# Phases rounded in PSUM, operands and background loads moved earlier, convolution strips in thirds

## The chip, the cores and the metric

One core of a Trainium2 chip (trn2) runs the kernel. The metric is the device time of one execution in microseconds (us). Line numbers in the profiles (L159) are those of the kernel profiled; the changed kernel has other numbers than the kernel before.

TensorE multiplies a stationary operand, loaded as weights, with a moving operand and writes to PSUM. ScalarE (ACT in the profile) does activations, VectorE (DVE) element-wise work, GpSimd (POOL) some element-wise work and, like SyncE (SP), issues DMA. An engine executes and issues in the order of its program: the timeline under e4 shows a store that is ready and leaves 4.8 us later, behind loads that wait. That order was set by a scheduler when the kernel was built, from the program order and the dependences.

## The reference, cut to what matters

Eight batches, a sequence of S = 5696, 128 channels:

```python
y = irfft(rfft(x, n=2*S) * rfft(h, n=2*S))[:, :S, :]     # a causal convolution per channel
theta = y @ w_theta
zr, zi = y * cos(theta), y * sin(theta)
u = y + einsum('ts,bsd->btd', w_tok_r, zr) + einsum('ts,bsd->btd', w_tok_i, zi)
out = u + relu(u @ w_ch)
```

The kernel computes the convolution as matmuls with Toeplitz strips of h. Then the *phases*: theta, its sine and cosine, zr and zi, for 45 tiles of 128 rows, of which 22 come first and 23 run in the background of the next stage. Then come the two 5696 x 5696 products, in a scheme with seven products in place of eight, in two passes over the sequence. Each pass works on *pairs* of output row tiles and keeps eleven *right operands* (zr and zi with five VectorE sums each) in SBUF. A pair is 154 matmuls of width 512 in four *stretches*; one piece of background work fits into each stretch.

## The kernel before: the parts that matter

The convolution: two strips per channel, four buffers.

```python
for k0, k1 in ((0, KS), (KS, NT)):                       # KS = 23, NT = 45
    strip = csb.tile([P, KS * P + 64], BF16, tag="strip")  # pool of 4
    nc.sync.dma_start(strip[:64, :w + 64], ...)            # 64 shifted rows of h_pad
    nc.vector.tensor_copy(strip[64:, :w], strip[:64, 64:w + 64])
    for k in range(k0, k1):
        nc.tensor.matmul(psum[...], strip[:, c:c + P], x_sb2[:, d, :B * ntj], ...)
```

The phases. `w_theta` is divided by 2 pi beforehand, so theta counts turns. Adding and taking away MAGIC = 1.5 * 2^23 rounds to whole turns and brings the argument of the sine into one turn:

```python
nc.tensor.matmul(theta_ps[...], yT[:, b, :], w_theta_sb, start=True, stop=True)   # per batch b
nc.scalar.activation(red, theta_ps, AF.Identity, bias=magic)                # theta + MAGIC
nc.vector.scalar_tensor_tensor(red, red, MAGIC, theta_ps, subtract, subtract)
nc.scalar.activation(mag, red, AF.Abs)
nc.scalar.activation(red, red, AF.Sin, ..., scale=-TWO_PI)                  # sine
nc.scalar.activation(mag, mag, AF.Sin, bias=half_pi, scale=-TWO_PI)         # cosine
zi_eng.tensor_mul(zi, red, yflat); nc.vector.tensor_mul(zr, mag, yflat)     # zi lies in red, zr in mag
for z, dst in ((zr, zr_hbm), (zi, zi_hbm)):
    nc.sync.dma_start(dst[ti]..., z)
```

All eleven right operands are loaded after the 22 tiles, 88 loads on SyncE. A background phase loads its `yb` in the slot that uses it, into one buffer, and TensorE transposes it at once. In pass two the four addends of a pair use four fixed buffers, from which the output is also stored:

```python
def first():                                   # background, third group of a stretch
    yb = cp.tile([P, 4, D], BF16, tag="yb")    # one buffer
    nc.sync.dma_start(yb..., half(y2_hbm, t, h))
    phases_a(yb, 0, yT, mps, 1)                # four transposes
...
c = cp.tile([P, 512], F32, tag=f"c{k}")        # addend and result, k = 0..3
```

## Time and profile before

| | before |
|---|---|
| median of 2 runs | 2746.23 us (2744.26 to 2748.20) |
| span of the profiled run | 2729.5 us |
| TensorE busy, granted clock | 83% of the span, 0.930 |
| VectorE, GpSimd, ScalarE busy | 61%, 31%, 23% |

This is the view of stretches for the kernel before. A line covers one stretch of time (from:to, its length), then for TensorE matmuls, weight loads, VectorE, ScalarE and GpSimd the busy us and the number of instructions, then the granted clock of TensorE, the busy share of the DMA engines and GB/s.

```profile
core 0: us, PE busy (x) PEld busy (x) DVE busy (x) ACT busy (x) POOL busy (x), PEclk, DMA share, GB/s
105.00:663.00 558.00, 484.56 (x5755) 410.61 (x5756) 230.67 (x256) 227.35 (x129) 0.00 (x0) 0.99 0.73 173
663.00:793.00 130.00, 40.99 (x365) 32.60 (x363) 89.56 (x98) 104.16 (x112) 17.34 (x32) 0.54 0.69 215
793.00:863.00 70.00, 46.70 (x162) 15.16 (x161) 51.93 (x94) 3.25 (x5) 14.27 (x25) 0.91 0.87 186
863.00:1811.00 948.00, 807.47 (x3727) 363.29 (x3726) 596.63 (x1121) 153.06 (x237) 442.23 (x757) 0.93 0.72 125
1811.00:1884.00 73.00, 47.86 (x159) 15.69 (x159) 52.15 (x98) 0.00 (x0) 17.19 (x32) 0.86 0.93 201
1884.00:2730.00 846.00, 792.02 (x4128) 373.22 (x4127) 578.10 (x1115) 102.66 (x180) 356.71 (x664) 0.99 0.74 126
```

The stretches are: the convolution; from its end to the first matmul of the first pair; the first pair; the rest of pass one; the first pair of pass two; the rest. (The load of x fills the first 105 us and is not touched by the change.) TensorE is meant to be the limit, but the second line has it busy for 41 of 130 us at clock 0.54, and the fourth for 807 of 948.

In the fourth, the loss lies where the background phases run (863 to 1440 us, eleven pairs). First the list of waits of TensorE there (who waited for whom; us in total, times, longest), then that stretch alone:

```profile
PE tpz L172 <- DMA yb<-y_hbm: 126.5, 42, 4.7
```

```profile
863.00:1440.00 577.00, 448.14 (x2056) 201.30 (x2056) 345.04 (x619) 146.26 (x225) 239.82 (x390) 0.89 0.63 116
```

The transposes wait 126.5 us for yb, and the clock is down to 0.89. The convolution's groups of instructions (count after the x, busy us, mean ns, then the idle time before them and who ended it) show TensorE waiting for the strips:

```profile
L159 PE MATMUL psum<-x_sb,strip 128*128 128x360 bf16 x5753 | 483.7, 244 | 73.4 <-DVE strip L148 37.4 <-DVE strip L154 34.7 <-ACT x_sb L119 1.1
```

The phases are carried by ScalarE. It is busy 104 of the 130 us, in 22 tiles with four ops of about 1.1 us each:

```profile
L191 ACT ACTIVATE red<-red,zero_b 128x1024 f32<-128x1024 f32 x22 | 25.0, 1138 | 0.1
L192 ACT ACTIVATE mag<-mag,half_pi 128x1024 f32<-128x1024 f32 x22 | 25.0, 1135 | 0.0
L186 ACT ACTIVATE red<-theta_ps,magic 128x1024 f32<-128x1024 f32 x22 | 24.0, 1108 | 12.6 <-DMA zi_hbm<-red 10.1 <-PE theta_ps L183 2.6
L190 ACT ACTIVATE mag<-red 128x1024 f32<-128x1024 f32 x22 | 22.5, 1047 | 1.3 <-DVE red L187 1.3
```

And in pass two, the chain of work that ended last (start, duration, what) goes in most pairs through an output store, the load of the next addend into the same buffer, and VectorE. One pair end as an example, then TensorE's busy time over 400 us of that pass:

```profile
by line: DMA out_dram<-c_19077 29.1%; DMA c_19442<-cp_hbm 17.1%; issue 6.6%; PE m_19803 L492 5.4%; DVE c_19077 L359 4.6%; DVE c_19446 L509 4.5%; PE m_19439 L492 4.4%; DVE c_19444 L511 4.1%; DVE c_19083 L359 4.0%; DVE c_19442 L510 4.0%; DVE 
...
2178.89 0.70 DVE c_19077 L359
...
2179.61 4.37 DMA out_dram<-c_19077
...
2183.99 2.57 DMA c_19442<-cp_hbm
...
2191.47 0.61 DVE c_19444 L511
...
2192.12 0.81 PE m_19803 L492 x3
```

```profile
2000.00:2400.00 400.00, 381.30 (x1985) 178.61 (x1985) 283.37 (x548) 48.61 (x85) 181.85 (x339) 1.00 0.79 133
```

### The profile page before, as it was taken

How to read it: one execution, taken by the hardware profiler on the slowest of the kernel's cores; microseconds unless marked ns; L12 is line 12 of the kernel's file. 1: busy time of each engine (PE TensorE's matmuls, PEld its weight loads, DVE VectorE, ACT ScalarE, POOL GpSimd, SP SyncE). 2: the span in 40 equal slices, each digit the busy share in tenths (PEclk: the TensorE clock that was granted, in tenths of full speed). 3: DMA queues.
4: the chain of work that ended last, by engine and by line, in shares of the span. 5: the costliest groups of instructions: out<-in, count | busy, mean ns of one | idle time of the engine just before them, and what ended most of it. 6: DMA issues, size and time to landing. Idle time of an engine off the chain costs nothing.

```text
span 2729.5 us, 38700 instructions
## 1 busy us (share of the span) xinstructions
PE 2269.4 (83%) x14422; PEld 1220.2 (45%) x14422; DVE 1663.5 (61%) x2842; ACT 636.6 (23%) x708; POOL 851.6 (31%) x1520
## 2 busy tenths in 40 slices
PE   4688888887347887777779999987999999999997
PEld 1377777776212333333334444433444444444443
DVE  5544434434767665565556677767776777667774
ACT  3444344435841222222220000000111111111111
POOL 0000000001002444344335655533444544444440
PEclk7699999999569998888889999999999999999998
DMA  9977777767858666566658978888777877787772
GB/s 249 225 179 176 171 178 175 177 169 181 263 158 165 116 133 118 105 114 120 107 105 138 154 129 133 134 167 172 132 130 135 140 126 133 129 138 134 129 131 61
DMA packets 431004, 404.64 MB, mean 148 GB/s; under 512 B 64480, under 2 KB 368864, under 8 KB 430688
## 3 DMA queue, kind: packets, MB, share of 16 engines
q0 software_dynamic: 222816, 131.33, 38.1%
q1 hardware_dynamic: 207568, 269.20, 36.4%
q8 instruction: 114, 1.87, 0.3%
q10 hardware_dynamic: 432, 1.64, 0.2%
q14 instruction: 74, 0.61, 0.1%
HBM read 448.22 MB, written 85.02 MB: 195 GB/s over the span
## 4 chain that ended last, share of the span: by engine, by line
PE 47%; DMA 28%; DVE 12%; ACT 4%; issue 4%; SPq 3%; POOL 1%; DVEq 0%; ACTq 0%; POOLq 0%
PE psum L159 10%; DMA strip<-h_pad 8%; DMA yb<-y_hbm 8%; DMA tmp<-in_x_dram 3%; SPq L258 2%; DVE mag L197 1%; DVE wt L284 1%; ACT red L191 1%; ACT mag L192 1%; DVE strip L148 1%; ACT mag L190 1%; ACT red L186 1%; PE tpz L172 1%; DVE strip L154 1%; PE utp L350 1%
## 5 line engine op out<-in xcount | busy, mean ns | idle before, releaser
L275 POOL DMA_DIRECT2D wb<-in_moe_w_tok_r_dram x720 | 388.5, 547 | 874.3 <-PE psum L159 659.5
L275 POOL DMA_DIRECT2D wb<-in_moe_w_tok_i_dram x720 | 388.9, 547 | 625.5 <-DVE wt L284 586.4
L159 PE MATMUL psum<-x_sb,strip 128*128 128x360 bf16 (+44 forms) x5760 | 483.9, 244 | 73.4 <-DVE strip L148 37.4
L159 PEld LDWEIGHTS <-strip 128*128 128x128 bf16 x5760 | 410.7, 98 | 147.3 <-DVE strip L148 43.8
L284 DVE STREAM_TRANSPOSE wt<-wb 128x384 f32<-128x384 f32 (+1 forms) x720 | 365.7, 527 | 162.9 <-DMA wb<-in_moe_w_tok_i_dram 25.7
L492 PEld LDWEIGHTS <-wt 128*128 128x128 bf16 x1936 | 191.9, 100 | 256.0 <-issue 40.9
L163 ACT ACTIVATE y_sb<-psum 128x360 bf16<-128x360 f32 x128 | 227.5, 1778 | 330.4 <-PE psum L159 330.4
L148 DVE COPY strip<-strip 64x2944 bf16<-64x2944 bf16 (+1 forms) x128 | 115.3, 904 | 164.4 <-DMA strip<-h_pad 148.9
L154 DVE COPY strip<-strip 64x2944 bf16<-64x2944 bf16 (+1 forms) x128 | 115.4, 906 | 160.5 <-DMA strip<-h_pad 141.3
L352 ACT ACTIVATE uts<-utp 128x512 bf16<-128x512 bf16 (+1 forms) x90 | 53.3, 592 | 571.1 <-PE utp L350 571.1
L196 POOL TENSOR_TENSOR red<-red,yb 128x512 bf16<-128x512 f32 x46 | 56.5, 1229 | 283.7 <-ACT red L191 274.6
L176 ACT ACTIVATE yT<-tpz 128x512 bf16<-128x512 bf16 x68 | 39.7, 594 | 420.3 <-PE tpz L172 420.3
L172 PE MATMUL tpz<-ident_bf,yb 128*128 128x128 bf16 x184 | 22.9, 263 | 126.7 <-DMA yb<-y_hbm 126.5
L187 DVE SCALAR_TENSOR_TENSOR red<-red,theta_ps 128x512 f32<-128x512 f32 (+1 forms) x68 | 58.0, 857 | 63.2 <-ACT red L186 62.8
L117 PE MATMUL rps<-tmpbf,R_bf 128*128 128x512 bf16 x90 | 46.5, 620 | 53.8 <-DVE tmpbf L114 53.5
L183 PE MATMUL theta_ps<-w_theta_sb,yT 128*128 128x128 bf16 x360 | 49.3, 284 | 50.1 <-ACT yT L176 47.2
L172 PEld LDWEIGHTS <-yb 128*128 128x128 bf16 x184 | 13.1, 113 | 149.5 <-DMA yb<-y_hbm 149.0
L114 DVE CAST tmpbf<-tmp 128x1024 bf16<-128x1024 f32 x45 | 56.5, 1261 | 34.5 <-DMA tmp<-in_x_dram 32.8
L347 ACT ACTIVATE ub<-c_16588 128x512 bf16<-128x512 f32 x1 | 0.6, 630 | 325.7 <-DVE c_16588 L511 325.7
L186 ACT ACTIVATE red<-theta_ps,magic 128x512 f32<-128x512 f32 (+1 forms) x68 | 55.6, 824 | 62.5 <-PE theta_ps L183 52.5
L183 PEld LDWEIGHTS <-yT 128*128 128x128 bf16 x360 | 33.7, 129 | 77.3 <-ACT yT L176 58.6
L190 ACT ACTIVATE mag<-red 128x512 f32<-128x512 f32 (+1 forms) x68 | 51.6, 766 | 37.7 <-DVE red L187 37.7
(6264 smaller groups left out, 4212.4 us busy)
## 6 DMA issues: line engine op xcount, KB each, us to landing
strip<-h_pad SPq DMA_DIRECT2D x128, 376.0 KB, 4.2
strip<-h_pad SPq DMA_DIRECT2D x128, 360.0 KB, 5.0
wb<-in_moe_w_tok_r_dram POOLq DMA_DIRECT2D x352, 96.0 KB, 4.4
wb<-in_moe_w_tok_i_dram POOLq DMA_DIRECT2D x352, 96.0 KB, 4.6
wb<-in_moe_w_tok_r_dram POOLq DMA_DIRECT2D x352, 80.0 KB, 4.1
wb<-in_moe_w_tok_i_dram POOLq DMA_DIRECT2D x352, 80.0 KB, 3.6
tmp<-in_x_dram SPq DMA_DIRECT2D x44, 512.0 KB, 5.8
y_hbm<-y_sb SPq DMA_DIRECT2D x45, 256.0 KB, 5.2
```

The costliest lines, as they stand in the source:

```text
L148: nc.vector.tensor_copy(strip[64:, :w], strip[:64, 64:w + 64])
L154: nc.vector.tensor_copy(strip[:64, 64:w + 64], strip[64:, :w])
L159: nc.tensor.matmul(psum[:, B * k: B * k + B * ntj], strip[:, c:c + P], x_sb2[:, d, :B * ntj], start=(k == 0), stop=(k == NT - 1))
L163: nc.scalar.activation(y_sb[:, :, :, d].rearrange("q t b -> q (t b)"), psum, AF.Copy)
L172: nc.tensor.transpose(tpz[:, b, :], y_ap[:, q + b, :], ident_bf)
L183: nc.tensor.matmul(theta_ps[:, b * D:(b + 1) * D], yT[:, b, :], w_theta_sb, start=True, stop=True)
L186: nc.scalar.activation(red, theta_ps, AF.Identity, bias=magic)
L187: nc.vector.scalar_tensor_tensor(red, red, MAGIC, theta_ps, op0=ALU.subtract, op1=ALU.subtract)
L190: nc.scalar.activation(mag, red, AF.Abs)
L275: nc.gpsimd.dma_start(wb[32 * i:32 * i + 32, :ng, :nj * 64], bass.AP(tensor=a.tensor, offset=a.offset + row0 * S + p * H + i * QR + j0 * 6 ...
L284: nc.vector.transpose(wt.rearrange("p j t r -> p (j t r)").bitcast(F32).rearrange("p (j g t) -> p g j t", j=TJ, g=4)[:, :ng, :nj], wb[:, : ...
L492: nc.tensor.matmul(ms[q], a[q][:, j, :, r], bts[jj][:, r, q, :], start=(jj == 0 and r == 0), stop=(jj == NJ - 1 and r == 1 and q not in left))
```

## The change

The change wants to take five kinds of waiting from TensorE at once. The convolution uses thirds of a strip and six buffers. For the first 22 tiles TensorE adds MAGIC, adds theta, takes MAGIC away and takes theta away again, all accumulated in PSUM, which removes one ScalarE op and one VectorE op per tile. The first four right operands get SBUF of their own and are loaded during the phases; of the other seven, ScalarE's queue issues half the loads. yb is loaded one slot ahead into two buffers. In pass two the addends rotate through six buffers. Two more moves go with it: the stores of y2 are issued by GpSimd, and the short pair of pass one moves from its end to its middle.

```diff
-    KS = 23
+    KS = 15
-    with tc.tile_pool(name="conv_sbuf", bufs=4) as csb, \
+    with tc.tile_pool(name="conv_sbuf", bufs=6) as csb, \
-            for k0, k1 in ((0, KS), (KS, NT)):
+            for k0 in range(0, NT, KS):
 ...
+            ones, plus, minus, w_neg = turns          # ones [1,128]; plus, minus [1,512] = +-MAGIC
+            for q in range(0, nb, 4):
+                bank = theta_ps[:, q * D:(q + 4) * D]
+                nc.tensor.matmul(bank, ones, plus, start=True, stop=False)
+                for b in range(q, q + 4):
+                    nc.tensor.matmul(theta_ps[:, b * D:(b + 1) * D], yT[:, b, :], w_theta_sb, start=False, stop=False)
+                nc.tensor.matmul(bank, ones, minus, start=False, stop=False)
+                for b in range(q, q + 4):
+                    nc.tensor.matmul(theta_ps[:, b * D:(b + 1) * D], yT[:, b, :], w_neg, start=False, stop=(b == q + 3))
+            r = theta_ps
+        nc.scalar.activation(mag, r, AF.Abs)
+        nc.scalar.activation(red, r, AF.Sin, bias=zero_b, scale=-TWO_PI)
 ...
+    def load_b(p, j, pool):
+            for z, s0, eng in ((zr_hbm, M2, nc.sync), (zi_hbm, M7, nc.sync if j < NE else nc.scalar)):   # NE = 4
 ...
-            nc.sync.dma_start(y2_hbm[ti], y_ap)
+                nc.gpsimd.dma_start(y2_hbm[ti], y_ap)
+            for j in range(max(0, 2 * a - 3), min(NE, 2 * a - 1)):      # after each round of tiles
+                load_b(0, j, bpe)
 ...
+            def load():
+                st["yb"] = yb = ybp.tile([P, 4, D], BF16, tag="yb", name="yb")   # pool of 2
+                nc.sync.dma_start(yb.rearrange("p b d -> p (b d)"), half(y2_hbm, t, h))
 ...
+            if p == 1:
+                tag = ("c0", "c1", "c2", "c3", "red", "mag")[tags["n"] % 6]
 ...
+        pairs = (list(range(11)) + [None] + list(range(11, 22)), list(range(22)) + [None])
 ...
-                    first, second = spread.pop(0)
+                    _, first, second = spread.pop(0)
                     first()
+                    if spread:
+                        spread[0][0]()                 # the load of the next slot
```

More of the change, by code (lines that the diff above doesn't have):

```diff
@@ L40 @@
     HW = Sp + P
-    KS = 23
+    KS = 15
+    assert NT % KS == 0
     BD = B * D
@@ L138 @@
             psum = cps.tile([P, NT * B], F32, tag="convps")
-            for k0, k1 in ((0, KS), (KS, NT)):
-                w = (k1 - k0) * P
+            for k0 in range(0, NT, KS):
+                k1 = k0 + KS
+                w = KS * P
                 j0 = P * k0
                 strip = csb.tile([P, KS * P + 64], BF16, tag="strip")
-                if d % 2 == 0:
-                    nc.sync.dma_start(strip[:64, :w + 64],
-                                      bass.AP(tensor=h_pad.tensor, offset=h_pad.offset + d * HW + j0,
-                                              ap=[[1, 64], [1, w + 64]]))
-                    nc.vector.tensor_copy(strip[64:, :w], strip[:64, 64:w + 64])
-                    c0 = 0
-                else:
-                    nc.sync.dma_start(strip[64:, :w + 64],
-                                      bass.AP(tensor=h_pad.tensor, offset=h_pad.offset + d * HW + j0,
-                                              ap=[[1, 64], [1, w + 64]]))
-                    nc.vector.tensor_copy(strip[:64, 64:w + 64], strip[64:, :w])
-                    c0 = 64
+                own, other, c0, c1 = ((slice(0, 64), slice(64, P), 0, 64) if d % 2 == 0 else
+                                      (slice(64, P), slice(0, 64), 64, 0))
+                nc.sync.dma_start(strip[own, :w + 64],
+                                  bass.AP(tensor=h_pad.tensor, offset=h_pad.offset + d * HW + j0,
+                                          ap=[[1, 64], [1, w + 64]]))
+                nc.vector.tensor_copy(strip[other, c0:c0 + w], strip[own, c1:c1 + w])
                 for k in range(k0, k1):
@@ L176, in phases_a, with phases_b @@
             nc.scalar.activation(yT[:, q:q + 4, :], tpz, AF.Copy)
-    def phases_b(ti, y_ap, b0, nb, yT, sb, th_pool, th_tag, zi_eng):
+    def phases_b(ti, y_ap, b0, nb, yT, sb, th_pool, th_tag, zi_eng, turns=None):
         n = nb * D
         theta_ps = th_pool.tile([P, n], F32, tag=th_tag, name="theta_ps")
-        for b in range(nb):
-            nc.tensor.matmul(theta_ps[:, b * D:(b + 1) * D], yT[:, b, :],
-                             w_theta_sb, start=True, stop=True)
         red = sb.tile([P, n], F32, tag="red")
-        nc.scalar.activation(red, theta_ps, AF.Identity, bias=magic)
-        nc.vector.scalar_tensor_tensor(red, red, MAGIC, theta_ps,
-                                       op0=ALU.subtract, op1=ALU.subtract)
         mag = sb.tile([P, n], F32, tag="mag")
-        nc.scalar.activation(mag, red, AF.Abs)
-        nc.scalar.activation(red, red, AF.Sin, bias=zero_b, scale=-TWO_PI)
+        if turns is None:
+            for b in range(nb):
+                nc.tensor.matmul(theta_ps[:, b * D:(b + 1) * D], yT[:, b, :],
+                                 w_theta_sb, start=True, stop=True)
+            nc.scalar.activation(red, theta_ps, AF.Identity, bias=magic)
+            nc.vector.scalar_tensor_tensor(red, red, MAGIC, theta_ps,
+                                           op0=ALU.subtract, op1=ALU.subtract)
+            r = red
+        else:
+            ones, plus, minus, w_neg = turns
[3 more added lines that the diff above has]
+                for b in range(q, q + 4):
+                    nc.tensor.matmul(theta_ps[:, b * D:(b + 1) * D], yT[:, b, :],
+                                     w_theta_sb, start=False, stop=False)
+                nc.tensor.matmul(bank, ones, minus, start=False, stop=False)
+                for b in range(q, q + 4):
+                    nc.tensor.matmul(theta_ps[:, b * D:(b + 1) * D], yT[:, b, :],
+                                     w_neg, start=False, stop=(b == q + 3))
+            r = theta_ps
+        nc.scalar.activation(mag, r, AF.Abs)
+        nc.scalar.activation(red, r, AF.Sin, bias=zero_b, scale=-TWO_PI)
         nc.scalar.activation(mag, mag, AF.Sin, bias=half_pi, scale=-TWO_PI)
@@ L220 @@
     wp = ctx.enter_context(tc.tile_pool(name="wpool", bufs=6))
-    tp = ctx.enter_context(tc.tile_pool(name="tpool", bufs=5))
-    sp = ctx.enter_context(tc.tile_pool(name="sumpool", bufs=4))
+    NE = 4
+    bpe = ctx.enter_context(tc.tile_pool(name="bpool_e", bufs=1, reuse_waits="tile"))
+    bts_of = {0: [], 1: []}
+    def load_b(p, j, pool):
+        bt = pool.tile([P, 2, 7, 512], BF16, tag=f"b{j}", name=f"b{j}")
+        for i in range(4):
+            r0 = p * H + i * QR + 64 * j
+            q = slice(32 * i, 32 * i + 32)
+            for z, s0, eng in ((zr_hbm, M2, nc.sync), (zi_hbm, M7, nc.sync if j < NE else nc.scalar)):
+                eng.dma_start(
+                    bt[q, :, s0:s0 + 2, :].rearrange("s r q n -> s r (q n)"),
+                    bass.AP(tensor=z.tensor, offset=z.offset + r0 * BD,
+                            ap=[[2 * BD, 32], [BD, 2], [1, BD]]))
+        b11, b12, b21, b22 = (bt[:, :, q, :] for q in (M2, M6, M7, M5))
+        nc.vector.tensor_sub(bt[:, :, M3, :], b12, b22)
+        nc.vector.tensor_sub(bt[:, :, M4, :], b21, b11)
+        nc.vector.tensor_add(bt[:, :, M1, :], b11, b22)
+        nc.vector.tensor_add(b12, b11, b12)
+        nc.vector.tensor_add(b21, b21, b22)
+        bts_of[p].append(bt)
@@ L224 @@
     with tc.tile_pool(name="s2", bufs=3, side="right") as sb1, \
+         tc.tile_pool(name="s2c", bufs=1, side="right") as sbc, \
          tc.tile_pool(name="s2p", bufs=2, space=bass.MemoryType.PSUM) as tps, \
          tc.tile_pool(name="s2q", bufs=3, space=bass.MemoryType.PSUM) as thp:
-        order = []
-        for a in range(6):
-            order += [t for t in (a, 5 + a, 11 + a, 16 + a) if t < 22 and t not in order]
-        for ti in order:
-            y_ap = y_sb[:, ti, :, :]
-            yT = sb1.tile([P, B, P], BF16, tag="yT")
-            for q in (0, 4):
-                phases_a(y_ap, q, yT, tps, q)
-            phases_b(ti, y_ap, 0, B, yT, sb1, thp, "th", nc.vector)
-            nc.sync.dma_start(y2_hbm[ti], y_ap)
@@ L237 @@
-        for ti in range(22, NT):
-            nc.sync.dma_start(y2_hbm[ti], y_sb[:, ti, :, :])
+        ones = sbc.tile([1, P], BF16)
+        nc.vector.memset(ones, 1.0)
+        plus = sbc.tile([1, 512], BF16)
+        nc.vector.memset(plus, MAGIC)
+        minus = sbc.tile([1, 512], BF16)
+        nc.vector.memset(minus, -MAGIC)
+        w_neg = sbc.tile([P, P], BF16)
+        nc.scalar.mul(w_neg, w_theta_sb, -1.0)
+        turns = (ones, plus, minus, w_neg)
+        seen = set()
+        for a in range(6):
+            for ti in (a, 5 + a, 11 + a, 16 + a):
+                if ti in seen or ti >= 22:
+                    continue
+                seen.add(ti)
+                y_ap = y_sb[:, ti, :, :]
+                yT = sb1.tile([P, B, P], BF16, tag="yT")
+                for q in (0, 4):
+                    phases_a(y_ap, q, yT, tps, q)
+                phases_b(ti, y_ap, 0, B, yT, sb1, thp, "th", nc.vector, turns)
+                nc.gpsimd.dma_start(y2_hbm[ti], y_ap)
+            for j in range(max(0, 2 * a - 3), min(NE, 2 * a - 1)):
+                load_b(0, j, bpe)
+            for ti in range(22 + 4 * a, min(NT, 26 + 4 * a)):
+                nc.gpsimd.dma_start(y2_hbm[ti], y_sb[:, ti, :, :])
@@ L239 @@
     ysb_ctx.close()
+    tp = ctx.enter_context(tc.tile_pool(name="tpool", bufs=5, reuse_waits="tile"))
+    sp = ctx.enter_context(tc.tile_pool(name="sumpool", bufs=4, reuse_waits="tile"))
     with tc.tile_pool(name="bpool", bufs=1, reuse_waits="tile") as bp, \
@@ L243 @@
          tc.tile_pool(name="wlpool", bufs=2, reuse_waits="tile") as wlp, \
+         tc.tile_pool(name="ybpool", bufs=2, reuse_waits="tile") as ybp, \
          tc.tile_pool(name="mps", bufs=1, space=bass.MemoryType.PSUM) as mps:
@@ L248, in half @@
             return z[ti].rearrange("p b d -> p (b d)")[:, h * 512:h * 512 + 512]
-        def load_b(p):
-            bts = []
-            for j in range(NJ):
-                bt = bp.tile([P, 2, 7, 512], BF16, tag=f"b{j}", name=f"b{j}")
-                for i in range(4):
-                    r0 = p * H + i * QR + 64 * j
-                    q = slice(32 * i, 32 * i + 32)
-                    for z, s0 in ((zr_hbm, M2), (zi_hbm, M7)):
-                        nc.sync.dma_start(
-                            bt[q, :, s0:s0 + 2, :].rearrange("s r q n -> s r (q n)"),
-                            bass.AP(tensor=z.tensor, offset=z.offset + r0 * BD,
-                                    ap=[[2 * BD, 32], [BD, 2], [1, BD]]))
-                b11, b12, b21, b22 = (bt[:, :, q, :] for q in (M2, M6, M7, M5))
-                nc.vector.tensor_sub(bt[:, :, M3, :], b12, b22)
-                nc.vector.tensor_sub(bt[:, :, M4, :], b21, b11)
-                nc.vector.tensor_add(bt[:, :, M1, :], b11, b22)
-                nc.vector.tensor_add(b12, b11, b12)
-                nc.vector.tensor_add(b21, b21, b22)
-                bts.append(bt)
-            return bts
         def load_w(a, row0, p, j0, nj, ng=4):
@@ L298, with nothing @@
         spread = []
+        def nothing():
+            pass
         def bg_phase(t, h):
             st = {}
+            def load():
+                st["yb"] = yb = ybp.tile([P, 4, D], BF16, tag="yb", name="yb")
+                nc.sync.dma_start(yb.rearrange("p b d -> p (b d)"), half(y2_hbm, t, h))
             def first():
-                st["yb"] = yb = cp.tile([P, 4, D], BF16, tag="yb", name="yb")
-                nc.sync.dma_start(yb.rearrange("p b d -> p (b d)"), half(y2_hbm, t, h))
+                yb = st["yb"]
                 st["yT"] = yT = cp.tile([P, 4, P], BF16, tag="yT", name="yT")
@@ L310, in second, with load @@
                 phases_b(t, st["yb"], 4 * h, 4, st["yT"], cp, mps, "misc", nc.gpsimd)
-            return first, second
+            return load, first, second
         def bg_left(g):
             n = min(4, NT - g)
-            def first():
-                wl = cp.tile([P, 4, 2, KL], BF16, tag="yb", name="wl")
+            st = {}
+            def load():
+                st["wl"] = wl = ybp.tile([P, 4, 2, KL], BF16, tag="yb", name="wl")
                 for r, a in enumerate((moe_w_tok_r, moe_w_tok_i)):
@@ L330, in first @@
                                     ap=[[S, S_last], [1, KL]]))
+            def first():
+                wl = st["wl"]
                 m = P if g + n < NT else S_last
@@ L339, in first @@
                 nc.sync.dma_start(wl_hbm[:, g:g + n, :m], wls[:, :n, :m])
-            return first, lambda: None
+            return load, first, nothing
         def u_stage(ti, h, c, m):
@@ L345, in first @@
             def first():
-                ub = cp.tile([P, 4, D], BF16, tag="yb", name="ub")
+                ub = ybp.tile([P, 4, D], BF16, tag="yb", name="ub")
                 nc.scalar.activation(ub[:m].rearrange("p b d -> p (b d)"), c[:m], AF.Copy)
@@ L364, in second @@
                     c[:m].rearrange("p (b d) -> p b d", b=4))
-            return first, second
+            return nothing, first, second
+        tags = {"n": 0}
         def addend(p, k, ti, h, m=P):
-            c = cp.tile([P, 512], F32, tag=f"c{k}", name=f"c{k}")
+            tag = f"c{k}"
+            if p == 1:
+                tag = ("c0", "c1", "c2", "c3", "red", "mag")[tags["n"] % 6]
+                tags["n"] += 1
+            c = cp.tile([P, 512], F32, tag=tag, name=f"c{k}")
             if p == 0:
@@ L381, in finish @@
                 spread.append(u_stage(ti, h, c, m))
-        bts_of, zl_of = {}, {}
+        zl_of = {}
         def start_pass(p):
-            bts_of[p] = load_b(p)
+            for j in range(len(bts_of[p]), NJ):
+                load_b(p, j, bpe if j < NE else bp)
             zl_of[p] = None
@@ L394, in start_pass @@
                 zl_of[p] = zl
-        chunks = [(p, tt, c) for p in range(2) for tt in list(range(22)) + [None]
-                  for c in range(len(CHUNKS))]
+        pairs = (list(range(11)) + [None] + list(range(11, 22)), list(range(22)) + [None])
+        chunks = [(p, tt, c) for p in range(2) for tt in pairs[p] for c in range(len(CHUNKS))]
         stretches = []
@@ L477 @@
                 ms = [mps.tile([P, 512], F32, tag=f"m{q}", name=f"m{q}") for q in range(7)]
-                where = ((tt, 0), (tt, 1), (22 + tt, 0), (22 + tt, 1))
+                where = ((tt, 1), (22 + tt, 0), (tt, 0), (22 + tt, 1))
                 cs = [addend(p, n, t, h) for n, (t, h) in enumerate(where)]
@@ L497 @@
                 if n == 1 and spread:
-                    first, second = spread.pop(0)
+                    _, first, second = spread.pop(0)
                     first()
+                    if spread:
+                        spread[0][0]()
                 if n == 4 and second is not None:
@@ L504 @@
                 continue
-            (c11, z11), (c12, z12), (c21, z21), (c22, z22) = cs
+            (c12, z12), (c21, z21), (c11, z11), (c22, z22) = cs
             nc.vector.tensor_add(c12, z12, ms[M3])
@@ L522 @@
         while spread:
-            first, second = spread.pop(0)
+            load, first, second = spread.pop(0)
             first()
```

## The prediction

> **What bounds the kernel now.** The table of stretches splits the 2729.5 us span (timed median 2746): loading x 105 us; convolution 558 us (105 to 663); phases of the first 22 tiles 122 us (to 785); right operands up to about 905 us; first pass with the remaining phases in its background 535 us (905 to 1440); rest of that pass 352 us; turn to pass two 83 us; pass two 815 us. TensorE is the intended limit, but it is at its pace only in parts: between 1525 and 1792 it is busy 99% at clock 1.00 (a 512-wide matmul every 0.216 us), between 905 and 1440 only 77% at clock 0.89.
>
> - Background: the list of waits charges TensorE 121.5 us there to transposes waiting for yb (median landing 5.2 us, a single buffer). After each wait matmuls start every 0.43 instead of 0.216 us. The Trainium skill, "TensorE: Matmul & The Clock Gate", Part 1, says an idle array drops to half clock and needs about 3.4 us of work to recover; the clock of 0.89 agrees and is worth another 50 to 60 us. A slot takes 13.05 us; its own TensorE work (38.5 matmuls and the background's) about 9.
> - Convolution: groups of 45 matmuls run in 3.8 us, a channel takes 4.36. TensorE waits 73 us for strip copies: a long half's buffer needs 2.85 us of matmuls, a 5 us load and a 0.9 us copy before it turns.
> - Phases: ScalarE is busy 104 of 122 us, four 1024-wide ops per tile (1.05 to 1.14 us) plus a copy; VectorE spends 26.4 us on the subtraction. Then 88 operand loads at 0.63 us each on one queue, 55 us, are in the chain of waits, with TensorE mostly idle.
> - Pass two: 1.7 us a pair waiting for VectorE's sums, whose addend load waits for an output store (both in the chain).
>
> **What the change does, per stage**
> - Strips in thirds, six buffers: the longest third needs about 1.9 us of matmuls, an estimated 4.2 us load and 0.65 us copy, inside the 7.6 us of two channels. Nearly TensorE bound; DMA share rises from 0.73 to about 0.84. Gain 55 us.
> - Phases: one ScalarE op (24 us) and one VectorE op (26 us) go; TensorE gets 8 more small and four 512-wide matmuls per tile. The stores stay (23 MB), and 4 MB of operand loads come in, so DMA holds it near 100 us. Seven operands remain after, issued from two queues, limited by VectorE's five sums each (0.65 us). From the end of convolution to full pace about 165 instead of 242 us: gain 75.
> - yb one slot ahead: the wait and the half clock go. DMA work per slot is 8.2 us (0.63 of 13.05) and VectorE 7.8, so I expect 10 us, not 9: gain 115 over 42 slots; 8 more with the left columns.
> - Turn between the passes (short pair moved away): 8. Addends in six buffers: 25.
>
> Sum 286 us; all are on the critical path. I take off some 10 for contention: **2470 us**, 80% range 2400 to 2560. Faster by over 2%: 0.96; within 2%: 0.03; slower 0.01.
>
> **What would show it.** Convolution about 505 us with no strip waits; no ScalarE identity op in the phases; yb gone from TensorE's waits and clock above 0.97 in the background; out and cp loads gone from the chain in pass two.
>
> **What would make it wrong.** Background paced by DMA, by VectorE or by the loop red, mag, store, red at 11 us or more; all y2 stores going out at once on GpSimd's queue and delaying the phase stores; TensorE at half clock becoming the phases' limit (about 5.4 us a tile); strip loads slowing as they get smaller.

## The result

| | before | after |
|---|---|---|
| median of 2 runs each | 2746.23 us | 2488.14 us (2485.04 to 2491.24) |
| ratio, 95% interval | | 0.906 (0.9004 to 0.9116) |
| span of the profiled run | 2729.5 us | 2489.4 us |
| TensorE busy, granted clock | 83%, 0.930 | 92%, 0.938 |

A ratio is the mean time of one kernel's runs over that of the other's of the same rounds, so it is not quite the ratio of the medians quoted. The profile of the kernel before is of a faster execution (2731 us) than its two timed ones, so gains read from the two profiles add up to about 17 us less than the medians show. The total is well inside the range on record (2400 to 2560). The view of stretches after the change, cut at the same events, shows that the parts are not as predicted:

```profile
core 0: us, PE busy (x) PEld busy (x) DVE busy (x) ACT busy (x) POOL busy (x), PEclk, DMA share, GB/s
105.00:599.00 494.00, 475.78 (x5763) 406.31 (x5762) 251.33 (x385) 227.74 (x130) 0.00 (x0) 0.99 0.79 198
599.00:733.00 134.00, 113.81 (x617) 57.48 (x618) 73.42 (x93) 80.58 (x91) 39.51 (x73) 0.51 0.71 220
733.00:795.00 62.00, 46.21 (x179) 17.11 (x178) 45.60 (x82) 7.71 (x12) 17.41 (x30) 0.88 0.94 192
795.00:1629.00 834.00, 769.07 (x3714) 349.81 (x3713) 592.67 (x1117) 143.50 (x231) 437.25 (x756) 0.97 0.81 143
1629.00:1696.00 67.00, 44.60 (x160) 15.79 (x159) 53.23 (x100) 0.00 (x0) 17.14 (x32) 0.90 0.98 208
1696.00:2489.00 793.00, 780.55 (x4127) 375.93 (x4125) 572.95 (x1114) 107.22 (x180) 356.28 (x664) 0.99 0.77 134
```

| part | before | after | gain | predicted |
|---|---|---|---|---|
| to the end of the convolution | 663 | 599 | 64 | 55 |
| end of the convolution to the first pair | 130 | 134 | -4 | together 75 |
| first pair | 70 | 62 | 8 | |
| rest of pass one | 948 | 834 | 114 | 115 + 8 |
| first pair of pass two | 73 | 67 | 6 | 8 |
| rest of pass two | 846 | 793 | 53 | 25 |
| sum | | | 241 | 286, less 10 |

The convolution lost nearly all of its waits; the loads of the thirds landed in 4.7 us (median) and the last column shows what is left:

```profile
L155 PE MATMUL psum<-x_sb,strip 128*128 128x360 bf16 (+44 forms) x5760 | 474.4, 243 | 17.8 <-DVE strip L151 16.4 <-ACT x_sb L120 1.1
```

In the background the wait for yb shrank and did not vanish, and the clock rose from 0.89 to 0.94:

```profile
PE tpz L168 <- DMA yb<-y_hbm: 50.0, 20, 4.8
PE tpz L168 <- DVE red L187: 11.9, 9, 3.7
```

```profile
795.00:1237.00 442.00, 378.82 (x1870) 171.83 (x1869) 314.77 (x566) 128.24 (x206) 218.65 (x361) 0.94 0.74 139
```

By the starts of pairs in the timelines, ten pairs of this stretch take 442 us, 44.2 us a pair; before, eleven pairs took 577 us, 52.4 us each. In pass two a pair fell from about 38.3 to 35.9 us, and TensorE is busy without a gap (before: 381 of the same 400 us). No output store and no addend load is left in the chain of that stage:

```profile
2000.00:2400.00 400.00, 400.00 (x2119) 192.22 (x2118) 298.33 (x579) 52.79 (x88) 191.41 (x358) 1.00 0.83 143
```

The phases are the surprise. ScalarE lost its op (busy 81 us, before 104), VectorE too, and still the stage takes longer, because TensorE now fills it. These are three of its five groups of matmuls in the phases, the products with w_theta and the two that add and take MAGIC (1x512: one row):

```profile
L196 PE MATMUL theta_ps<-w_theta_sb,yT 128*128 128x128 bf16 x176 | 27.3, 310 | 4.8 <-DVE yT L170 3.2 <-ACT yT L172 0.9
...
L198 PE MATMUL theta_ps<-minus,ones 1*128 1x512 bf16 x44 | 26.5, 602 | 0.0
...
L194 PE MATMUL theta_ps<-plus,ones 1*128 1x512 bf16 x44 | 25.0, 606 | 5.3 <-ACT red L204 5.3
```

Each is 25 to 27 us, and the transposes and the products with -w_theta are as long; a one-row matmul of width 512 takes 0.60 us here, no less than one with all 128 rows at the same clock (0.61 us, the first two of the first pair). The stage as one stretch has TensorE busy 116 of 136 us at a clock of 0.51:

```profile
599.00:735.00 136.00, 115.81 (x622) 58.22 (x623) 75.42 (x94) 81.31 (x91) 39.51 (x73) 0.51 0.71 219
```

### The profile page after: what moved, and what is told of

It is laid out like the page before. It is cut to its first block, busy times and chain, and to the rows that moved or that the text cites. A ratio compares the mean times of both kernels' runs of the same rounds, so it can differ in the third digit from the quotient of the medians.

```text
span 2489.4 us, 39835 instructions
## 1 busy us (share of the span) xinstructions
PE 2279.7 (92%) x14686; PEld 1232.4 (50%) x14686; DVE 1653.3 (66%) x2951; ACT 612.4 (25%) x687; POOL 871.5 (35%) x1565
## 4 chain that ended last, share of the span: by engine, by line
PE 63%; DMA 20%; DVE 9%; POOL 3%; issue 3%; ACT 2%; SPq 0%; DVEq 0%; ACTq 0%; POOLq 0%
PE psum L155 13%; DMA strip<-h_pad 6%; DMA yb<-y_hbm 3%; DMA tmp<-in_x_dram 2%; POOL wb L304 2%; DMA zi_hbm<-red 2%; DMA wb<-in_moe_w_tok_r_dram 2%; DMA wb<-in_moe_w_tok_i_dram 1%; DMA h_bf<-in_h_dram 1%; DVE wt L313 1%; DVE mag L210 1%; DVE strip L151 1%; PE utp L389 1%; PE tpz L168 1%; PE v L396 1%
## 5 line engine op out<-in xcount | busy, mean ns | idle before, releaser
L155 PE MATMUL psum<-x_sb,strip 128*128 128x360 bf16 (+44 forms) x5760 | 474.4, 243 | 17.8 <-DVE strip L151 16.4
L313 DVE STREAM_TRANSPOSE wt<-wb 128x384 f32<-128x384 f32 (+2 forms) x720 | 362.4, 525 | 127.4 <-PE m_13363 L510 11.3
L151 DVE COPY strip<-strip 64x1920 bf16<-64x1920 bf16 x384 | 250.7, 654 | 240.3 <-DMA strip<-h_pad 207.8
L186 ACT ACTIVATE red<-theta_ps,magic 128x512 f32<-128x512 f32 x46 | 31.6, 688 | 252.7 <-DMA zi_hbm<-red 228.9
L210 DVE TENSOR_TENSOR mag<-mag,yb 128x512 bf16<-128x512 f32 x46 | 50.6, 1101 | 50.5 <-ACT mag L205 50.5
L120 ACT ACTIVATE x_sb<-rps 128x1024 bf16<-128x1024 f32 x45 | 46.1, 1024 | 57.1 <-PE rps L118 56.6
L205 ACT ACTIVATE mag<-mag,half_pi 128x512 f32<-128x512 f32 (+1 forms) x68 | 58.0, 853 | 0.0
L118 PEld LDWEIGHTS <-R_bf 128*128 128x128 bf16 x90 | 6.2, 111 | 88.5 <-DVE tmpbf L115 79.6
L203 ACT ACTIVATE mag<-red 128x512 f32<-128x512 f32 x46 | 29.0, 630 | 82.0 <-DMA zr_hbm<-mag 46.4
```

Source lines behind the costliest of these rows:

```text
L151: nc.vector.tensor_copy(strip[other, c0:c0 + w], strip[own, c1:c1 + w])
L155: nc.tensor.matmul(psum[:, B * k: B * k + B * ntj], strip[:, c:c + P], x_sb2[:, d, :B * ntj], start=(k == 0), stop=(k == NT - 1))
L313: nc.vector.transpose(wt.rearrange("p j t r -> p (j t r)").bitcast(F32).rearrange("p (j g t) -> p g j t", j=TJ, g=4)[:, :ng, :nj], wb[:, : ...
```

## The experiments

The theory after reading the two traces: (1) the convolution, the background and pass two gained by the mechanisms predicted, each from its own part of the change; (2) the phases gained nothing because TensorE, at half clock, is now their limit; (3) what is left in the background comes from SyncE's queue. Rivals are told with each run. The kernel before had a median of 2740.35, 2735.79 and 2744.20 us in the three batches (7 runs each), so kernels of different batches are compared by their ratio to it. The change itself has 0.906, which is about 2483 us against 2740. Its interval is wide (two runs), so differences of a few us rest on stages in the profiles and on the other runs of the same batch. The profiles have a spread too: among the runs that left the background alone (e2, e3, e6, e7, e10 and the change) its stage took 524 to 534 us. Two parts of the change have no run of their own: the short pair's move and the second queue for seven operands.

The stages of all runs, from their profiles, in us: phases (end of the convolution to the last VectorE product of the 22 tiles), background (from there to the last background transpose, first pair included), pass two (first to last output transpose).

| run | median | ratio (95%) | phases | background | pass two |
|---|---|---|---|---|---|
| before | 2746.2 | | 119 | 651 | 836 |
| the change | 2488.1 | 0.906 (0.9004 to 0.9116) | 135 | 534 | 783 |
| e1 thirds only | 2676.2 | 0.9763 (0.9736 to 0.979) | 121 | 656 | 839 |
| e2 no turn | 2481.6 | 0.905 (0.9025 to 0.9074) | 134 | 526 | 783 |
| e3 y2 on SyncE | 2480.0 | 0.9045 (0.9022 to 0.9068) | 131 | 530 | 783 |
| e4 stores on ScalarE | 2453.1 | 0.8945 (0.8922 to 0.8968) | 133 | 495 | 783 |
| e10 full rows | 2464.8 | 0.9003 (0.8982 to 0.9025) | 120 | 524 | 783 |
| e5 no prefetch | 2585.5 | 0.9452 (0.9427 to 0.9476) | 134 | 620 | 783 |
| e6 old tags | 2531.3 | 0.9253 (0.9229 to 0.9278) | 135 | 533 | 837 |
| e7 loads behind stores | 2468.8 | 0.9016 (0.8995 to 0.9037) | 123 | 526 | 783 |
| e11 all late | 2477.2 | 0.9033 (0.8991 to 0.9075) | 120 | 542 | 783 |
| c3 | 2436.8 | 0.8882 (0.884 to 0.8925) | 108 | 505 | 783 |
| c4 | 2437.1 | 0.8878 (0.8824 to 0.8932) | 97 | 522 | 783 |
| c6 | 2448.5 | 0.893 (0.8888 to 0.8973) | 127 | 495 | 783 |

All gave correct results.

### e1: the strips alone

The kernel before with this part of the diff only:

```diff
-    KS = 23
+    KS = 15
-    ... bufs=4 ... for k0, k1 in ((0, KS), (KS, NT)):
+    ... bufs=6 ... for k0 in range(0, NT, KS):
```

> The kernel before with the convolution strips in thirds and nothing else. Theory: the whole convolution gain of the change (558 to 496 us in the two profiles) comes from this part alone, because a strip buffer now turns within two channels; expected 2746 - 62 = about 2684 us, the strip waits of TensorE near 16 us instead of 73, all later stages as before. Rival: the gain is smaller when the stores of the next stage are placed as before; then over 2710.

It took 2676 us, 64 less than the kernel before of its batch, and the convolution went from 556 to 487 us, with the other stages 2 to 5 us longer. The strips give the whole gain of that stage and nothing elsewhere.

### e2: the rounding back on ScalarE and VectorE

```diff
-                phases_b(ti, y_ap, 0, B, yT, sb1, thp, "th", nc.vector, turns)
+                phases_b(ti, y_ap, 0, B, yT, sb1, thp, "th", nc.vector)
```

> The change, with the rounding of the phases back on ScalarE and VectorE (no accumulation of the magic number in PSUM). Theory: the phase stage (601 to 735 us after) is paced by TensorE at half clock, some 4.3 us of matmuls a tile plus waits, so moving the rounding there won nothing; undone, the stage takes about the same, 125 to 140 us, and the total stays within 12 us of 2488. Rival: ScalarE is still the limit and the two ops taken off it were worth 24 us; then the stage is 155 us or more and the total about 2510 to 2515.

The phases took 134 us, as with the rounding in PSUM, and the ratio is 0.905 against 0.906. As the change stands, moving the rounding to TensorE is worth nothing. Both expected numbers came out, but that does not test the reason given for them, since in e2 another engine sets the pace (stretch of e2):

```profile
601.00:735.00 134.00, 44.68 (x365) 34.49 (x366) 99.04 (x116) 105.33 (x113) 39.49 (x73) 0.57 0.72 221
```

TensorE is busy for 45 of the 134 us, ScalarE for 105. Two different limits happen to give the same length.

### e3: the y2 stores back on SyncE

```diff
-                nc.gpsimd.dma_start(y2_hbm[ti], y_ap)
+                nc.sync.dma_start(y2_hbm[ti], y_ap)
```

and the same for the tiles from 22 on.

> The change, with the 45 y2 stores issued by SyncE again in place of GpSimd. Theory: on GpSimd all 11.5 MB leave at once at the start of the phases and hold the first zi and zr stores for 9 to 10 us each (622 to 643 us, ScalarE waits for their buffers); interleaved on SyncE with the phase stores that wait goes, the stage shrinks by 10 to 20 us, total about 2470 to 2478. Rival: the bytes have to go in any case and the wait only moves; then within 5 us of 2488.

The total of 2480 us lies between the two expectations, and the stage shrank by 4 us only, where 10 to 20 were expected, so the store wait is not what holds it. The trace is of use all the same. With the stores out of the way, TensorE has hardly a gap in the middle of the phases, and its clock stays at half (stretch of e3):

```profile
640.00:700.00 60.00, 54.67 (x300) 27.68 (x298) 33.70 (x42) 34.10 (x40) 0.00 (x0) 0.50 0.58 196
```

In 60 us TensorE is busy 91% at a mean granted clock of 0.50.

### e10: the same matmuls with all 128 rows

```diff
-        ones = sbc.tile([1, P], BF16)
-        plus = sbc.tile([1, 512], BF16)
-        nc.vector.memset(plus, MAGIC)
+        ones = sbc.tile([P, P], BF16)
+        plus = sbc.tile([P, 512], BF16)
+        nc.vector.memset(plus, MAGIC / P)
```

and `minus` likewise. 128 rows of MAGIC / 128 sum to MAGIC exactly, and the number and width of the matmuls stay.

> The change, with the matmuls that add and take the magic number using all 128 rows (ones 128x128, the constant divided by 128, exact in bf16 and in the sum) where the change uses one row. Number and width of the matmuls stay, so at one clock they take the same time. Theory: the granted clock stays at 0.50 through the phases, although TensorE is busy nearly all the time there, because one-row matmuls (1.7 of some 4.3 us a tile) hardly count as activity; with full rows the clock goes to 0.9 or more and the phase stage from 134 to 100 to 115 us, total 2455 to 2470. Rival: the clock depends on the share of time alone, or on the small matmuls with gaps between them; it stays near 0.5 and the total within 5 us of 2485.

```profile
599.00:718.00 119.00, 66.53 (x607) 45.91 (x620) 73.16 (x92) 80.28 (x91) 39.42 (x73) 0.81 0.83 249
```

This is the stretch of the phases of e10. Against the change's the granted clock went from 0.51 to 0.81, TensorE's busy time from 116 to 67 us for the same work, and the stage from 135 to 120 us. The total fell by about 16 us by the ratios (0.906 to 0.9003; the two intervals overlap), which is within the band expected by time; the stage was expected at 100 to 115 us and the clock at 0.9 or more, and neither was quite reached. All other matmuls, the transposes among them, were the same in both runs. So the half clock was a limit of the phases, and the one-row matmuls were what kept it half. That the granted clock follows the number of rows in use is the reading that suggested the run; the run does not tell it from other ways in which a 128-row matmul is heavier.

### e5: no load ahead

```diff
-         tc.tile_pool(name="ybpool", bufs=2, reuse_waits="tile") as ybp, \
+         tc.tile_pool(name="ybpool", bufs=1, reuse_waits="tile") as ybp, \
             def first():
+                load_now()                             # what load() did
                 yb = st["yb"]
-            return load, first, second
+            return nothing, first, second
```

> The change, with yb loaded in its own slot into a single buffer as in the kernel before. Theory: the load one slot ahead is most of what the background gained; without it the transposes wait for yb again, 120 us or so in all, and the clock falls; total 2485 + 80 to 100 = about 2575. Rival: the SyncE queue behind the pair's end holds the background either way, and the load was only part: +30 to 50 us.

It cost 107 us by the ratios (0.9452 less 0.906, of 2740) and 97 by the medians, the upper end of the band or a little over it, and the background stage went from 534 to 620 us. The wait of the transposes is back at nearly what it was before, as the list of waits of e5 shows:

```profile
PE tpz L168 <- DMA yb<-y_hbm: 117.7, 43, 4.7
```

So the load ahead, with its second buffer, is the largest part of the change (e1: 64 us, e6: 53 us).

### e6: four fixed addend buffers again

```diff
-            if p == 1:                 # six tags in turn
+            if p == 2:                 # never
```

> The change, with the addends of pass two back in four fixed buffers (order of loads as changed). Theory: pass two shrank by 53 us in the profiles (836 to 783) because an addend's load no longer waits for the output store of the pair before; undone, pass two is 825 to 840 and the total about 2530. Rival: part of the 53 us comes from the changed order of the four addends, then pass two is 800 to 815 us.

Pass two went back to 837 us (before: 836), and the wait of TensorE on VectorE's sums came back:

```profile
PE m L539 <- DVE c L560: 25.5, 15, 1.7
```

The six buffers give all of the 53 us. The changed order of the four addends gives nothing that can be seen while there are four buffers.

### e7 and e11: no loads during the phases

```diff
-            for j in range(max(0, 2 * a - 3), min(NE, 2 * a - 1)):
+            for j in ():
```

> The change, with all eleven right operands loaded after the phases (no load during them; the second queue for seven of them stays). Theory: the phases lose the 32 loads, their DMA traffic and 20 VectorE sums and get 5 to 10 us shorter, the start of pass one gets 25 to 30 us longer (32 loads of 0.63 us on SyncE plus landing and sums); total +15 to +22 us. Rival: the early loads only moved time into the phases, total within 5 us of 2485.

The run came out faster than the change, by about 12 us by the ratio, where both theories had it slower or equal. It also did not undo what it was meant to undo. The four operands still had SBUF of their own, so the scheduler moved their loads into the phases anyway, one or two at a time behind the stores. In the change the eight loads of the third operand stand in a row on SyncE (issued from 677.1 to 682.5 us), ahead of the next zr and zi stores. What e7 shows is that the place of the loads in the program cost about 12 us, which is also what the phases lost (135 to 123). How it did so is not shown. That stores were held up behind the loads is the obvious reading, but ScalarE's waits for these stores in the phases come to 6 us in the change and to 7 in e7. The second run takes the SBUF away, so that nothing can be loaded before y_sb is free:

```diff
-    NE = 4
-    bpe = ctx.enter_context(tc.tile_pool(name="bpool_e", bufs=1, reuse_waits="tile"))
+    NE = 0
+    bpe = None
```

> The change, with no operand kept in a place of its own: all eleven right operands lie where y_sb lay and can only be loaded once the phases are over (each zr part from SyncE, each zi part from ScalarE). The run e7 was meant to show this and did not: the scheduler moved its loads into the phases all the same, only behind the stores on the queue, and it was 16 us faster than the change. Theory: loading during the phases is worth something by itself; all late, the phases take about 115 to 120 us, but the first pass starts 20 to 25 us later against them than in e7; total 2480 to 2495. Rival: the loads during the phases were worth nothing; total 2470 or less.

At 2477 us it lies between the theory and the rival, and its ratio of 0.9033 lies between the change and e7, with intervals that overlap both. Loading four operands during the phases, as the change does it, brought nothing that can be seen: what the start of pass one gained was paid in the phases. The phases of e11 have practically no operand loads in them (the first is issued at 718.6 us), and they show TensorE at half clock as the limit (stretch of e11):

```profile
601.00:721.00 120.00, 111.22 (x626) 56.40 (x621) 64.45 (x79) 80.62 (x91) 41.62 (x77) 0.52 0.73 216
```

TensorE is busy 111 of 120 us at a clock of 0.52, in 22 tiles about 5.4 us each. The waits that its list shows there come to 4 us.

### e4: the background's stores on a queue of their own

The change's background has a new wait. Its timeline at the end of a pair (start, duration, engine, line, instruction; in brackets the idle time before it and who ended it):

```profile
915.51 0.32 SPq L212 DMA_DIRECT2D zr_hbm<-mag  x1
...
916.29 1.17 POOL L209 TENSOR_TENSOR red<-red,yb 128x512 bf16<-128x512 f32 x1
...
919.31 0.32 SPq L417 DMA_DIRECT2D yy_10608<-y_hbm  x1
...
921.89 0.32 SPq L417 DMA_DIRECT2D yy_10611<-y_hbm  x1
...
922.30 0.38 SPq L212 DMA_DIRECT2D zi_hbm<-red  x1
...
922.78 0.38 SPq L337 DMA_DIRECT2D yb<-y_hbm  x1
...
926.01 0.69 ACT L186 ACTIVATE red<-theta_ps,magic 128x512 f32<-128x512 f32 x1 [11.26 <-DMA zi_hbm<-red]
...
927.57 0.38 PE L168 MATMUL tpz<-ident_bf,yb 128*128 128x128 bf16 x4 [1.92 <-DVE red L187]
```

The product zi is done at 916.29 + 1.17 = 917.46 us, but its store leaves SyncE only at 922.30, because four yy loads stand before it that wait for VectorE's sums. When the store has landed, at about 926, ScalarE writes the next red after 11.26 us of waiting, and TensorE's next transposes wait for the PSUM buffer. The edit:

```diff
-            nc.sync.dma_start(dst[ti]..., z)
+            (st_eng or nc.sync).dma_start(dst[ti]..., z)      # st_eng=nc.scalar in the background
```

> The change, with the background's zi and zr stores issued by ScalarE instead of SyncE. Theory: at the end of each pair the zi store sits on SyncE's queue about 5 us behind four yy loads that wait for VectorE's sums; ScalarE's next red then waits 10 us for the store to land, PSUM stays taken and the next yb transposes wait. With the stores on a queue of their own a pair of the background takes about 37 to 39 us instead of 42.5: total 2488 - 40 = 2440 to 2460. Rival: DMA and VectorE pace the background, the queue does not matter: within 8 us of 2488.

It gained 31 us by the ratios, within the band; the background stage went from 534 to 495 us, and a pair of it takes 39.8 us, where 37 to 39 were expected. TensorE's wait for yb, whose loads stood behind these stores, fell from 50 to 30 us. ScalarE's waits for these stores, first the change, then e4:

```profile
ACT red L186 <- DMA zi_hbm<-red: 226.4, 43, 11.3
ACT mag L203 <- DMA zr_hbm<-mag: 46.4, 18, 5.7
```

```profile
ACT red L186 <- DMA zi_hbm<-red: 108.0, 21, 7.5
...
ACT mag L203 <- DMA zr_hbm<-mag: 31.8, 16, 2.4
```

The queue's order was worth half of that wait. The other half is taken to be the store's own time in a loop with one buffer each for red and mag, which no run shows: a second pair of buffers did not fit into SBUF beside the rest (it failed to build), so that was not tried on the chip. A pair without background work takes 33.7 us (after the change, 1359 to 1629 us), so part of theory (3), that the rest comes from SyncE's queue, stays open: e4's pairs still take 39.8 us.

### c3, c4 and c6: together

c3 takes the edits of e4, e10 and e7; c4 adds that of e3; c6 is c3 with that of e2 and without e10's, which it does not need.

> Three amendments together: full rows for the magic number (e10), the background's stores on ScalarE's queue (e4), the early loads behind the stores (e7). If the gains of 19, 30 and 16 us were independent: 2485 - 65 = 2420. The full rows and the late loads both shorten the phases, so part of them should overlap: 2420 to 2435.

> As c3, with the y2 stores on SyncE besides. With TensorE no longer at half clock the phases may now be held by stores, so the first zi and zr stores no longer sharing the DMA engines with all of y2 could bring 5 to 10 us that e3 could not show (it brought 4). Rival: in order of issue the y2 stores now push the operand loads to the end of the phases, and it loses 5 to 15 us against c3.

> As c3, but with the rounding of the phases on ScalarE and VectorE as before, so that c3 against c6 is what rounding in PSUM is worth once TensorE is warm. Theory: the two ops taken off (24 us of ScalarE in 22 tiles) now count, c6 is 10 to 20 us slower than c3. Rival: stores and loads pace the phases either way; within 5 us of c3.

c3 takes 2437 us (0.8882), about 49 us less than the change and 11% less than before. It was expected at 2420 to 2435, so it just missed. The three gains of 31, 16 and 12 us add up to 59. The expectation had the phases' two gains overlap, but the stages show them whole: 27 us, as e10's 15 and e7's 12. What is missing lies at the start of pass one: the background is 505 us against 495 in e4, though a pair of it takes 40 us in both, and from the end of the phases to the second pair's first transposes it is 77 us against 70. Its phases:

```profile
601.00:709.00 108.00, 63.13 (x612) 43.49 (x621) 71.47 (x89) 80.95 (x91) 39.49 (x73) 0.87 0.88 270
```

c4 has the shortest phases of all, 97 us, and the same total, so neither of its expectations came true in the total. Its background is 17 us longer than c3's, which is where the rival looked for the loss. c6 is 12 us slower by medians. The intervals of the two ratios overlap, but all four runs of c6 (2445 to 2454 us) are slower than all four of c3 (2430 to 2440) in the same batch, so rounding in PSUM is worth about 12 us once the matmuls use all rows. The phases differ by 19 us (108 and 127), and 10 of them come back in the background (505 and 495).

## Why the prediction was right in the sum and wrong in one step

- **Convolution**: predicted 55, measured 64. The mechanism was the one named, and e1 isolates it. The residual waits were 16 us.
- **Background**: predicted 115 over 42 slots and 8 for the left columns, measured 114 for the rest of pass one. e5 shows that the load ahead is the cause. That 114 is so near to 115 is partly luck: a slot (a quarter of a pair) fell from 13.1 to 11.05 us and not to 10, so the ten pairs gained 82 us, and the other 32 came later in the pass. Two marks of the prediction were missed here: yb was to be gone from TensorE's waits (50 us are left) and the clock above 0.97 (0.94). The warning of the prediction about the loop red, mag, store, red came true in part: ScalarE waited 226 us on zi stores, and e4 took off 31 us of it.
- **Pass two**: predicted 25, measured 53 (e6: all of it the buffers). The term was mis-sized: the prediction took the 1.7 us that the list of waits showed for one instruction of each pair, 37 us in 22 pairs, and discounted it to 25, while a pair lost 2.4 us (38.3 against 35.9). From start to start of the matmuls (six pairs, 2074 to 2304 us), the gap at the sums costs 1.75 us a pair, and the other 0.6 us are smaller gaps, mostly around the products of the output stage. They went too. The distance between the starts of two pairs counts them all.
- **Phases and start of pass one: this step failed.** The prediction had "From the end of convolution to full pace about 165 instead of 242 us: gain 75". Measured from the end of the convolution to the second pair it is 200 before and 196 after, a gain of 4; to the third pair, nearer to the prediction's mark, 249 and 236. Three things stood in its place. First, TensorE took over the phases at half clock: e10 and e11. The prediction had this case in its list of what would make it wrong, with 5.4 us a tile, and e11 measures 5.4, but its sum was made with DMA as the limit. Second, the place of the operand loads in the phases cost about 12 us: e7, by a way that stays open. Third, the seven late operands were "limited by VectorE's five sums each (0.65 us)", an estimate of about 23 us in all (7 x 5 x 0.65), but one landed every 6.2 us. This is SyncE's timeline after the change (three of the seven groups of loads):

```profile
737.75 4.66 SPq L244 DMA_DIRECT2D b_8840<-zr_hbm  x4
742.54 5.59 SPq L244 DMA_DIRECT2D b_8854<-zr_hbm  x4
749.35 5.70 SPq L244 DMA_DIRECT2D b_8868<-zr_hbm  x4
```

Before the change, with one queue, an operand landed every 6.0 us, so the second queue brought no speed. The likely reason is that the DMA engines were nearly full there: the share of the third stretch after the change is 0.94 at 192 GB/s (before: 0.87 at 186). No run takes the second queue away alone.
- The total was right, 2488 against 2470, partly by luck: of the 71 us that the start did not give, about half was made good by 28 us more in pass two and 9 in the convolution, and the range took the rest. A total inside its range does not confirm the terms; only the stages do.

On what the Trainium skill says: "TensorE: Matmul & The Clock Gate", Part 1, has the clock go to full after about 3.4 us of sustained activity. The background is in keeping with it (clock 0.89 with 126.5 us of waits; 1.00 where TensorE never waits, as from 2000 to 2400 us after the change). The phases are not: 60 us at 91% busy stayed at 0.50 in e3, and here the measurement decides. "DMA: Bandwidth & Descriptors", section "Issuing engines are not separate DMA queues", says that issuing from several engines saves only the time of the sequencers. That agrees with the seven operands, which landed one per 6.2 us from two queues and one per 6.0 us from one. For e4 the sequencer was the point: the same page, "Anatomy of one DMA — SWDGE (gpsimd) path", says that a semaphore wait happens on the issuing sequencer before dispatch. It says so under the path of GpSimd; SyncE behaved in the same way here, where such waits held a finished tile's store for 4.8 us.

## What to carry to other kernels

Before moving work to an idle engine, cost it at the clock which that engine will be granted in that stage, and look at how heavy its instructions are and not only at how long they fill the time: here work moved to TensorE was worth nothing until it used all rows. A load brought forward has a place in the program, and the place has a price (about 12 us in e7), so try more than one. Give stores that others wait for a queue on which nothing stands that waits for another engine. Predict by stages with marks that can be read in both traces, since errors in the terms cancel in the sum.

## What the Trainium skill lacked or had wrong

- "TensorE: Matmul & The Clock Gate", Part 1, ties the full clock to time busy. Here TensorE was busy 91% of 60 us at a granted clock of 0.50 (e3), with one-row matmuls of width 512 among matmuls of width 128. The phases of the change, which have the same matmuls, had 0.51; with 128 rows in those of width 512 they had 0.81 (e10). The page makes an exception of transposes (Part 4), but those were the same in both runs; it does not say that the number of rows bears on the clock.
- "Perfetto Trace Analysis", "DMA Optimizations", advises to give loads and stores to different issuing engines, above all with loops or control flow. It has no figure and does not name the case met here: a store that was ready waited 4.8 us behind loads that were not, and moving these stores to another engine's queue gained 31 us (e4).
